# Clamping weight exponents on VectorE instead of ScalarE, wider spacing of the sums of second weights, and another order in the last product, in an fp32 attention and two-layer MoE kernel on one core

## The chip, the cores and the metric

The kernel runs on one NeuronCore of a Trainium2 chip, as one launch. The metric is the time of one launch on the device, in microseconds (us), as the median of several runs. TensorE is written PE, VectorE DVE, ScalarE ACT, GpSimd POOL and the queue that issues the transfers SP. PEld is PE's weight load, which runs beside its matmuls.

## The reference, cut to what matters

The inputs are `x` (4 batches, 8 heads, 512 tokens, 64 wide), a `state` of 32 tokens per batch, and the weights. TOK = 4 x (512 + 32) = 2176 tokens of 512 numbers go through the two layers.

```
a  = softmax(x @ state^T / 8);  xread = a  @ state
a2 = softmax(state @ x^T / 8);  sread = a2 @ x
x  = concat(xread, sread), heads side by side            # 2176 x 512
h  = x @ w_in                                            # 512 x 2048, float64
x  = (max(h, 0) + alpha * min(h, 0)) @ w_out             # 2048 x 512, float64
P  = exp(x @ w_gate - max), scaled 8 times by rows and columns
out = sum over 8 experts e of P[:, e] * (max(x @ w1[e], 0) @ w2[e])   # 512 x 1024 x 512
```

`w_in` and `w_out` are float64, so the kernel gets them as 64-bit words and has to make float32 of them on the chip. Each float32 product is made of three products of a shorter format: every operand is split into a high part and a low part (`...h`, `...l`), and high x high, high x low and low x high are summed in PSUM.

## The kernel before, in words

**Weights of the first layer.** F1 = 2048 is cut in eight steps u of 256. A step's weights, `w_in` and `w_out` together, are four pieces (u, j) of 128 x 512 words of 64 bits. `to_f32` (L98) turns one piece into float32 on three engines. DVE takes the exponent's bits out of the upper half word into `y` (L109) and later joins the lower bits (L115) and the sign (L123). ACT scales the low half word (L112) and clamps the exponent in three passes over `y`: max(y - 14336, 0) (L113), max(4095 - y, 0) (L119), and back times 2^19 (L120). POOL adds exponent and mantissa (L121). `split_w` (L129) then makes the high part on ACT (L138) and the low part on POOL (L139). There are 32 pieces.

**Start.** `start` (L1299) and the first part of the program (step 0, and step 1 up to the second product of the first batch) leave the order of each engine to a scheduler in the build. In this part run the attention of the four batches (`read_x`, L234) and the conversions of the first two steps. `read_x` of a batch makes the scores `psc` (L250), maxima and exponentials, sums (L271 to L273), the normalisation on POOL (L275), transposes `pat` (L282) whose halves go out on ACT and DVE (L230, L231), and then transposes `pst` (L295) for the softmax the other way. `pat` and `pst` share two PSUM banks, so `pst` waits until L231 has read `pat`.

**First layer.** From there on each engine follows the order of the code, which is dealt out in slots: a slot is a group of matmuls (`layer1` L503 or `layer2_first` L541), and after each slot every lane of side work (conversions `w`, attention `x`, and so on) takes one step. `layer1` is followed by ACT L527, DVE L530, ACT L535 and POOL L536, which make `gh` and `gl`. `layer2_first` fills a PSUM bank `po` (L551, three banks) and DVE adds it to the sum `acc` (L568). The conversion of step u + 1 is spread over step u by `weights` (L1276).

**Experts.** The 8 experts are 32 steps of 256, walked for each of three groups of tokens: 96 steps s. First products are done with seven smaller products (`quad`, `px`, `py`, `pz`, L850). Second products are plain in group 0 (L1167) and done with seven smaller products in groups 1 and 2 (`product`, L1023), from sums of second weights that are made in group 0 on ACT (L798) and DVE (L800) and kept in DRAM. For six steps these sums are made apart, in a lane of their own (`apart`, L815): it starts at step 6, and at step 26 what is left of it is done at once. `sums_b(u, raw, home, gap, rest)` (L776) takes `gap` and `rest` as the slots that it leaves free.

**The end.** `finish_last` (L1084) does the last second product plainly, joins the seven products' sums (five on DVE, two on POOL), transposes them and adds both. Tiles are cut where the six chunks of tokens end: (128, 128, 64) and (64, 128, 128) rows. Three tiles `pe` of the plain product run first, in three banks. Then come all transposes `pt`, each tile copied out by ACT (L1127), then the other three tiles of the plain product. DVE adds `pe` and the copy (L1109), and a transfer stores the tile.

Of the kernel before, what the change touches and what calls it, by code (L numbers as in the profile page):

```python
# [8 lines left out]
F32 = mybir.dt.float32  # L9
F32R = mybir.dt.float32r  # L10
I32 = mybir.dt.int32
# [3 lines left out]
AF = mybir.ActivationFunctionType  # L15
ALU = mybir.AluOpType
# [28 lines left out]
def body(ctx: ExitStack, tc: tile.TileContext, xt_in, xn_in, stb, stk, wd, ws, alpha, wgate, out):  # L45
# [22 lines left out]

    ident = const.tile([P, P], F32, name="ident")
    ones = const.tile([P, P], F32, name="ones")  # L70
    rebias = const.tile([P, 1], F32, name="rebias")
    full = const.tile([P, 1], F32, name="full")
    alpha_sb = const.tile([P, F1 // P], F32, name="alpha_sb")
    beta = const.tile([P, F1 // P], F32, name="beta")
    wg_raw = const.tile([P, KD, E], F32, name="wg_raw")
# [24 lines left out]
    def to_f32(u, j):  # L100

        w = raw_t[u, j].bitcast(I32).rearrange("p (n two) -> p n two", two=2)
        s = raw_t[u, j].bitcast(U16).rearrange("p (n four) -> p n four", four=4)
        lo_w, hi_w = w[:, :, 0], w[:, :, 1]
        y = rawp.tile([P, 512], F32, tag="y", name=f"y{u}_{j}", bufs=2)
        nc.vector.tensor_scalar(  # L109
            out=y.bitcast(I32), in0=hi_w, scalar1=16, scalar2=0x7FFF, op0=ALU.logical_shift_right, op1=ALU.bitwise_and  # L110
        )
        nc.scalar.activation(out=lo_w, in_=lo_w.bitcast(U32), func=AF.Copy, scale=2.0**-29)  # L112
        nc.scalar.activation(out=y, in_=y.bitcast(I32), func=AF.Relu, bias=rebias)  # L113
        yield
        nc.vector.scalar_tensor_tensor(  # L115
            out=lo_w, in0=s[:, :, 2], scalar=8.0, in1=lo_w, op0=ALU.mult, op1=ALU.add
        )

        nc.scalar.activation(out=y, in_=y, func=AF.Relu, scale=-1.0, bias=full)  # L119
        nc.scalar.activation(out=y.bitcast(I32), in_=y, func=AF.Copy, scale=-float(1 << 19), bias=4095.0 * (1 << 19))  # L120
        nc.gpsimd.tensor_tensor(out=lo_w, in0=y.bitcast(I32), in1=lo_w, op=ALU.add)  # L121
        yield
        nc.vector.scalar_tensor_tensor(  # L123
            out=lo_w, in0=hi_w, scalar=-0x80000000, in1=lo_w, op0=ALU.bitwise_and, op1=ALU.bitwise_or
        )
        src_t[u, j] = f32(lo_w)
# [688 lines left out]
    def apart():  # L815

        load_apart(None)
        yield 16
        for u in APART:
            yield from sums_b(u, raw_apart[u], "xl4", 2, 12)  # L820

    left2, whole = {}, {}

# [224 lines left out]
    def store(g, h, t0, nt, t):  # L1048

        tok = CH[2 * g + h][0] + t0  # L1050
        if tok < B * S:
            r0 = tok // S * (S + NS) + tok % S
            nc.sync.dma_start(out=out[r0:r0 + nt, :], in_=t[:nt])
        else:
            for b in range(B):
                r0 = b * (S + NS) + S
                nc.sync.dma_start(out=out[r0:r0 + NS, :], in_=t[b * NS:(b + 1) * NS])

    def cuts(g, h):

        t0, end = CH[2 * g + h][0], CH[2 * g + h][0] + CH[2 * g + h][1]
        at = t0
        while at < end:
            n = min(P, end - at, B * S - at if at < B * S else P)
            yield at - t0, n
            at += n
# [14 lines left out]
    def join(eng, g, x, y):  # L1081
        eng.tensor_tensor(out=mm[g][x], in0=mm[g][x], in1=mm[g][y], op=ALU.add)

    def finish_last(g):  # L1084

        s = NS2 - 1
        stage = big.tile([P, 6, DM], F32, tag="acc0", name="stage")
        gh, gl = g2[s]
        wh, wl = second[s]
        n = CH[2 * g][1]  # L1090
        parts = [(h, t0, nt) for h in range(2) for t0, nt in cuts(g, h)]

        def plain(i):
            h, t0, nt = parts[i]
            ps = ps_h.tile([P, 512], F32, tag="h", name=f"pe{i}")
            k = 0
            for f in range(NF):
                for x, w in ((gl, wh), (gh, wh), (gh, wl)):
                    nc.tensor.matmul(
                        ps[:nt], lhsT=x[:, f, h * n + t0:h * n + t0 + nt], rhs=w[:, f, :],  # L1100
                        start=(k == 0), stop=(k == 3 * NF - 1),
                    )
                    k += 1
            return ps

        def close(i, ps):
            h, t0, nt = parts[i]
            t = stage[:nt, i, :]
            nc.vector.tensor_tensor(out=t, in0=ps[:nt], in1=t, op=ALU.add)  # L1109
            store(g, h, t0, nt, stage[:, i, :])  # L1110

        for eng, x, y in (
            (nc.gpsimd, "P2", "P1"), (nc.gpsimd, "P3", "P5"), (nc.vector, "P6", "P1"), (nc.vector, "P7", "P6"),
            (nc.vector, "P4", "P7"), (nc.vector, "P3", "P6"), (nc.vector, "P7", "P5"),
        ):
            join(eng, g, x, y)
        first_ps = [plain(i) for i in range(3)]
        for i in range(0, 6, 2):
            ps = p2["m"].tile([P, 2, 512], F32, tag="m", name=f"pt{i}")
            for j in range(2):  # L1120
                h, t0, nt = parts[i + j]
                blocks = [("P2", "P4"), ("P3", "P7")][h]
                for k in range(KD):
                    nc.tensor.transpose(
                        ps[:nt, j, k * P:(k + 1) * P], mm[g][blocks[k // 2]][:, k % 2, t0:t0 + nt], ident
                    )
                nc.scalar.activation(out=stage[:nt, i + j, :], in_=ps[:nt, j], func=AF.Copy)  # L1127
        for i in range(3):
            close(i, first_ps[i])
        for i in range(3, 6):  # L1130
            close(i, plain(i))

    spread = {}

# [164 lines left out]
    def start():  # L1299
        load_b(0)  # L1300
        for j in range(2):
            load_w(0, j)
        make_identity(nc, ident)
        nc.vector.memset(ones, 1.0)
        nc.vector.memset(rebias, -14336.0)
        nc.vector.memset(full, 4095.0)
        warm(10)
        load_b(1)
        load_w(0, 2)
        load_b(2)  # L1310
        for j in range(2):
            load_w(1, j)
        load_b(3)
        load_w(1, 2)
        nc.sync.dma_start(out=alpha_sb, in_=alpha)
        nc.sync.dma_start(out=wg_raw, in_=wgate)

        x0, x1 = read_x(0), read_x(1)
        w0 = early([(0, j) for j in range(NPIECE)])
        for task in (x0, x1, x0, x0, w0, x0, w0, x0, w0, x0, w0):  # L1320
            next(task)
        for b in range(B):
            make_st2(b)
        next(w0)
        warm(30)
        nc.vector.tensor_scalar(out=beta, in0=alpha_sb, scalar1=-1.0, scalar2=1.0, op0=ALU.mult, op1=ALU.add)
        lanes["x"] += [x0, x1, read_x(2), read_x(3)]
        lanes["state"] += [states(b) for b in range(B)]
        lanes["w"] += [w0, early([(1, j) for j in range(NPIECE)])]
        lanes["v"] += [make_v(0), make_v(1)]  # L1330
# [201 lines left out]
```

## Time and profile before

| what | us |
|---|---|
| median of three runs (1857.4 to 1863.1) | 1859.85 |
| the profiled execution | 1864.35 |
| its span, first to last instruction | 1862.5 |
| PE busy in the span | 1791.9 (96%) |
| DVE busy | 1507.0 (81%) |
| POOL busy | 1252.4 (67%) |
| ACT busy | 732.8 (39%) |

The span is the stretch that the profiler's records cover; 1.85 us of the profiled execution lie outside it. Busy shares are means over the whole span: what an engine has free in one stage is read from windows of that stage. In the trace a row gives the start, the duration, the engine, the line of the kernel and the operands; in brackets stands how long the engine had been idle before it, and which instruction ended that.

### The profile page before, as it was taken

What the parts mean: (1) busy time and instruction counts of PE and PEld (TensorE: products, weight loads), DVE (VectorE), ACT (ScalarE), POOL (GpSimd) and SP (SyncE); (2) the same over time, 40 slices, a digit from 0 to 9 for tenths busy, and PEclk for the clock granted to TensorE, in tenths of its full rate; (3) what the DMA queues carried; (4) which work ended last, traced back from release to release, by engine and by line L of the source; (5) the groups of instructions that cost most, each with busy time, mean ns of one, the idle gap of its engine ahead of it and who ended that gap; (6) DMA issues with size and microseconds to landing.
All of it is one profiled execution on the core that took longest, in us unless ns stands there. A gap on an engine that the chain in (4) does not pass through costs nothing.

```text
span 1862.5 us, 29291 instructions
## 1 busy us (share of the span) xinstructions
PE 1791.9 (96%) x10173; PEld 1662.6 (89%) x10173; DVE 1507.0 (81%) x2318; ACT 732.8 (39%) x1394; POOL 1252.4 (67%) x1297
## 2 busy tenths in 40 slices
PE   6799999999989999999999999999999999999998
PEld 5688788877878888888889999999999999999997
DVE  6744777776899999998997777777788888877786
ACT  6755666654323443343332222222223333233332
POOL 4523555566667777787647777777776898677774
PEclk8899999999999999999999999999999999999998
DMA  6111111122659899898797677767777787888883
GB/s 221 46 52 46 57 46 57 46 74 84 235 210 332 329 331 326 321 333 299 271 332 271 252 269 269 256 254 250 266 263 266 265 308 278 325 312 315 296 305 106
DMA packets 153026, 427.20 MB, mean 229 GB/s; under 512 B 17312, under 2 KB 34208, under 8 KB 152880
## 3 DMA queue, kind: packets, MB, share of 16 engines
q1 hardware_dynamic: 152880, 425.34, 63.2%
q8 instruction: 81, 1.33, 0.3%
q14 instruction: 65, 0.53, 0.1%
HBM read 302.28 MB, written 122.99 MB: 228 GB/s over the span
## 4 chain that ended last, share of the span: by engine, by line
PE 69%; DVE 16%; POOL 4%; issue 4%; DMA 3%; ACT 3%; SPq 1%; DVEq 0%; POOLq 0%; ACTq 0%
PE pm L1023 22%; PE py L850 11%; PE px L850 8%; PE pz L850 8%; PE po L551 7%; PE po L1167 5%; PE ph L522 4%; DVE oa L1189 2%; DVE wz L800 2%; DVE g2l L873 1%; POOL w2l L672 1%; DMA kept_bs<-wz 1%; PE pv L484 1%; DVE c L857 1%; DMA rw<-in_ws_dram 1%
## 5 line engine op out<-in xcount | busy, mean ns | idle before, releaser
L1029 DVE TENSOR_TENSOR m<-pm,m 128x768 f32<-128x768 f32 (+1 forms) x427 | 377.9, 886 | 124.7 <-PE pm L1023 124.7
L1023 PE MATMUL pm<-formgh,wz 128*128 128x384 f32 (+1 forms) x1134 | 212.7, 322 | 0.4 <-DVE m L1029 0.4
L850 PE MATMUL px<-rB,wah 128*128 128x384 f32 (+1 forms) x768 | 189.9, 329 | 3.8 <-DVE g2l L873 3.5
L954 POOL TENSOR_TENSOR formgh<-mid,formgh 128x384 fp32r<-128x384 f32 (+1 forms) x126 | 121.2, 962 | 106.2 <-ACT formgh L953 106.1
L850 PE MATMUL py<-rT,wsh 128*128 128x384 f32 (+1 forms) x768 | 188.1, 327 | 0.2 <-DVE u L857 0.2
L1023 PEld LDWEIGHTS pm<-formgh,wz 128*128 128x128 f32 x1134 | 186.7, 188 | 0.7 <-issue 0.7
L672 POOL TENSOR_TENSOR w2l<-rw,w2h 128x512 fp32r<-128x512 f32 x64 | 87.0, 1381 | 127.9 <-ACT w2h L670 118.1
L536 POOL TENSOR_TENSOR gl<-r,gh 128x512 fp32r<-128x512 f32 (+1 forms) x80 | 94.3, 1192 | 114.8 <-ACT gh L535 60.2
L872 ACT ACTIVATE g2h<-c 128x384 fp32r<-128x384 f32 x96 | 50.5, 526 | 305.8 <-DVE c L857 305.8
L1167 PE MATMUL po<-w2l,g2h 128*128 128x512 f32 x384 | 152.4, 397 | 0.0
L1167 PE MATMUL po<-w2h,g2h 128*128 128x512 f32 x384 | 151.6, 395 | 0.0
L1167 PE MATMUL po<-w2h,g2l 128*128 128x512 f32 x384 | 150.0, 391 | 0.4 <-DVE g2l L873 0.4
L850 PEld LDWEIGHTS px<-rB,wah 128*128 128x128 f32 x768 | 135.7, 189 | 13.2 <-DVE g2l L873 8.1
L850 PEld LDWEIGHTS py<-rT,wsh 128*128 128x128 f32 x768 | 136.0, 188 | 3.6 <-DVE u L857 0.6
L964 POOL TENSOR_TENSOR T<-mid,mid 128x384 f32<-128x384 f32 (+1 forms) x126 | 118.0, 959 | 30.8 <-DVE mid L938 30.0
L953 ACT ACTIVATE formgh<-mid 128x384 fp32r<-128x384 f32 (+1 forms) x126 | 63.0, 500 | 178.1 <-DVE mid L938 134.2
L551 PE MATMUL po<-gl,wh 128*128 128x512 f32 (+1 forms) x320 | 120.1, 376 | 13.1 <-DVE acc L568 11.3
L1189 DVE SCALAR_TENSOR_TENSOR oa<-po,pr,oa 128x512 f32<-128x512 f32 x168 | 124.3, 740 | 6.8 <-PE po L1167 6.0
L938 DVE SCALAR_TENSOR_TENSOR mid<-mid,pb 128x384 f32<-128x384 f32 (+1 forms) x192 | 123.3, 642 | 6.6
L850 PE MATMUL px<-rB,wal 128*128 128x384 f32 (+1 forms) x384 | 125.6, 327 | 0.0
L850 PE MATMUL py<-rT,wsl 128*128 128x384 f32 (+1 forms) x384 | 125.2, 326 | 0.0
L1023 PE MATMUL pm<-formgl,w2h 128*128 128x384 f32 (+1 forms) x504 | 121.2, 323 | 3.4 <-DVE m L1029 1.9
(259 smaller groups left out, 5169.6 us busy)
## 6 DMA issues: line engine op xcount, KB each, us to landing
wz<-kept_bs SPq DMA_DIRECT2D x126, 512.0 KB, 8.1
kept_bs<-wz SPq DMA_DIRECT2D x64, 512.0 KB, 6.1
wsh<-kept_as_h SPq DMA_DIRECT2D x64, 512.0 KB, 3.7
wsl<-kept_as_l SPq DMA_DIRECT2D x64, 512.0 KB, 6.1
wah<-kept_a_h SPq DMA_DIRECT2D x64, 384.0 KB, 2.9
wal<-kept_a_l SPq DMA_DIRECT2D x64, 384.0 KB, 4.3
w2h<-kept_b_h SPq DMA_DIRECT2D x63, 384.0 KB, 6.5
w2l<-kept_b_l SPq DMA_DIRECT2D x63, 384.0 KB, 7.1
```

Of the source, the lines that this page charges most:

```text
L522: nc.tensor.matmul(ps, lhsT=w, rhs=x, start=(i == 0), stop=(i == len(terms) - 1))
L536: nc.gpsimd.tensor_tensor(out=lo, in0=r, in1=f32(hi), op=ALU.subtract)
L551: nc.tensor.matmul(ps, lhsT=w2(wt, u, f, d * P, P), rhs=g[:, f, :n], start=(i == 0), stop=(i == 3 * NF - 1))
L672: nc.gpsimd.tensor_tensor(out=lo[:, i], in0=src[:, i], in1=f32(hi[:, i]), op=ALU.subtract)
L850: nc.tensor.matmul(bank[b], lhsT=w[:, k * P:(k + 1) * P], rhs=xf[:, j, k, :], start=(first and i == 0), stop=(i == 5), skip_group_check=True,)
L938: nc.vector.scalar_tensor_tensor(out=out, in0=src, scalar=0.0, in1=pb[:, e % 2, h * n:(h + 1) * n], op0=ALU.max, op1=ALU.mult)
L954: nc.gpsimd.tensor_tensor(out=lo, in0=out, in1=f32(hi), op=ALU.subtract)
L964: nc.gpsimd.tensor_tensor(out=out, in0=x, in1=y, op=ALU.subtract)
L1023: nc.tensor.matmul(ps[:, q, :n], lhsT=w[:, q * P:(q + 1) * P], rhs=x, start=(j == 0), stop=(j == 2))
L1029: nc.vector.tensor_tensor(out=mm[g][name], in0=ps[:, :, :n], in1=mm[g][name], op=ALU.add)
L1167: nc.tensor.matmul(ps, lhsT=x[:, f, t * P:(t + 1) * P], rhs=w[:, f, :], start=(i == 0), stop=(i == 3 * NF - 1))
L1189: nc.vector.scalar_tensor_tensor(out=a, in0=ps, scalar=p, in1=a, op0=ALU.mult, op1=ALU.add)
```

## The change

It has three parts. In `to_f32` the three ACT passes over `y` give way to two integer passes on DVE, in place: add -14336 and take the larger of that and 0, then take the smaller of that and 4095 and multiply by 2^19. Two constants and their memsets go. In `apart` the slots left free are 4 and 14 in place of 2 and 12. `finish_last` does the plain product for five whole tiles of 128 rows first, copied out by ACT; the joins write one tile `blocks` with the rows side by side; then five tiles are transposed, and DVE adds each transposed bank to the copy. Five tiles are stored, the last by four transfers of 32 rows. Lines below the first part move up by 2.

```diff
@@ to_f32
-        nc.scalar.activation(out=y, in_=y.bitcast(I32), func=AF.Relu, bias=rebias)
+        yi = y.bitcast(I32)
+        nc.vector.tensor_scalar(out=yi, in0=yi, scalar1=-14336, scalar2=0, op0=ALU.add, op1=ALU.max)
         yield
         nc.vector.scalar_tensor_tensor(
             out=lo_w, in0=s[:, :, 2], scalar=8.0, in1=lo_w, op0=ALU.mult, op1=ALU.add
         )
-        nc.scalar.activation(out=y, in_=y, func=AF.Relu, scale=-1.0, bias=full)
-        nc.scalar.activation(out=y.bitcast(I32), in_=y, func=AF.Copy, scale=-float(1 << 19), bias=4095.0 * (1 << 19))
+        nc.vector.tensor_scalar(out=yi, in0=yi, scalar1=4095, scalar2=1 << 19, op0=ALU.min, op1=ALU.mult)
         nc.gpsimd.tensor_tensor(out=lo_w, in0=y.bitcast(I32), in1=lo_w, op=ALU.add)
@@ apart
-            yield from sums_b(u, raw_apart[u], "xl4", 2, 12)
+            yield from sums_b(u, raw_apart[u], "xl4", 4, 14)
@@ finish_last
-        stage = big.tile([P, 6, DM], F32, tag="acc0", name="stage")
+        t0, nt = GT[g]
+        stage = big.tile([P, nt, DM], F32, tag="acc0", name="stage")
+        whole_t = big.tile([P, KD, 2 * n], F32, tag="acc1", name="blocks")
+        def block(i, h):
+            return whole_t[:, 2 * i:2 * i + 2, h * n:(h + 1) * n]
+        for eng, to, x, y in (
+            (nc.gpsimd, block(0, 0), "P2", "P1"), (nc.gpsimd, m["P3"], "P3", "P5"), (nc.vector, m["P6"], "P6", "P1"),
+            (nc.vector, m["P7"], "P7", "P6"), (nc.vector, block(1, 0), "P4", "P7"),
+            (nc.vector, block(0, 1), "P3", "P6"), (nc.vector, block(1, 1), "P7", "P5"),
+        ):
+            eng.tensor_tensor(out=to, in0=m[x], in1=m[y], op=ALU.add)
...
-        first_ps = [plain(i) for i in range(3)]
-        for i in range(0, 6, 2):
...
-        for i in range(3):
-            close(i, first_ps[i])
-        for i in range(3, 6):
-            close(i, plain(i))
+        for t in range(nt):
+            ps = bank(("tr", "m", "h", "h", "h")[t], f"pe{t}")
...
+            nc.scalar.activation(out=stage[:, t, :], in_=ps, func=AF.Copy)
+        for t in range(nt):
+            ps = bank(("m", "tr", "m", "h", "h")[t], f"pt{t}")
+            for k in range(KD):
+                nc.tensor.transpose(ps[:, k * P:(k + 1) * P], whole_t[:, k, t * P:(t + 1) * P], ident)
+            row = stage[:, t, :]
+            nc.vector.tensor_tensor(out=row, in0=ps, in1=row, op=ALU.add)
...
+                nc.sync.dma_start(out=out[r0:r0 + P, :], in_=row)
```

Three places show how it moves instructions. A row names line, operation, result and operands. In the names `raw1_3` is piece (1, 3), `wl` a low half of weights, `r1_0` the row sums of batch 1, and `early_a`, `early_b` hold the pieces (1, 0) to (1, 2) and the exponentials of the batches 0 and 1.

POOL in the start, before, from the piece (0, 2) on:

```order
L139 TENSOR_TENSOR wl0_2_386<-raw0_2_136,wh0_2_385 128x512
L275 TENSOR_TENSOR early_b_102<-early_b_102,r1_0_473 128x512
L275 TENSOR_TENSOR early_b_102<-early_b_102,r1_1_478 128x512
L214 TENSOR_TENSOR stl_100<-xt3_0_145,sth_99 128x2x64 x2
L121 TENSOR_TENSOR raw0_3_252<-y0_3_259,raw0_3_252 128x512
L121 TENSOR_TENSOR early_a_101<-y1_0_427,early_a_101 128x512
L139 TENSOR_TENSOR wl0_2_386<-raw0_3_252,wh0_2_385 128x512
L121 TENSOR_TENSOR early_a_101<-y1_1_435,early_a_101 128x512
L139 TENSOR_TENSOR wl1_0_449<-early_a_101,wh1_0_448 128x512
L121 TENSOR_TENSOR early_b_102<-y1_2_444,early_b_102 128x512
L139 TENSOR_TENSOR wl1_0_449<-early_a_101,wh1_0_448 128x512
L121 TENSOR_TENSOR raw1_3_281<-y1_3_457,raw1_3_281 128x512
```

And POOL at the same place with the change (L119, L137, L273 and L534 are the former L121, L139, L275 and L536):

```order
L119 TENSOR_TENSOR raw0_3_246<-y0_3_252,raw0_3_246 128x512
L119 TENSOR_TENSOR early_a_99<-y1_0_419,early_a_99 128x512
L137 TENSOR_TENSOR wl0_2_378<-raw0_3_246,wh0_2_377 128x512
L119 TENSOR_TENSOR early_a_99<-y1_1_426,early_a_99 128x512
L137 TENSOR_TENSOR wl1_0_439<-early_a_99,wh1_0_438 128x512
L119 TENSOR_TENSOR early_b_100<-y1_2_434,early_b_100 128x512
L137 TENSOR_TENSOR wl1_0_439<-early_a_99,wh1_0_438 128x512
L273 TENSOR_TENSOR early_b_100<-early_b_100,r1_0_461 128x512
L119 TENSOR_TENSOR raw1_3_274<-y1_3_446,raw1_3_274 128x512
L137 TENSOR_TENSOR wl1_2_597<-early_b_100,wh1_2_596 128x512
L273 TENSOR_TENSOR early_b_100<-early_b_100,r1_1_466 128x512
L534 TENSOR_TENSOR gl0_0_336<-r0_0_1_391,gh0_0_335 128x512
```

The two normalisations of batch 1 (`r1_0`, `r1_1`), which stood ahead of the conversions from (0, 3) on, now stand behind seven and nine instructions of conversions; the second half of `gl0_0` stands right behind them.

PE in the start, before, from batch 1's transposes on:

```order
L282 MATMUL pat1_0_483<-ident_87,early_b_102 128x128 x4
L282 MATMUL pat1_1_490<-ident_87,early_b_102 128x128 x4
L295 MATMUL pst1_0_497<-ident_87,sc1_0_402 128x128 x2
L295 MATMUL pst1_0_497<-ident_87,sc1_1_403 128x128 x2
L295 MATMUL pst1_1_506<-ident_87,sc1_0_402 128x128 x2
L295 MATMUL pst1_1_506<-ident_87,sc1_1_403 128x128 x2
L250 MATMUL psc2_0_515<-xt2_0_138 128x64 x8
L551 MATMUL po0_0_0_645<-gl0_0_344,wh0_2_385 128x512
L551 MATMUL po0_0_0_645<-gh0_0_343,wh0_2_385 128x512
```

And with the change (L280, L293 and L549 are the former L282, L295 and L551):

```order
L549 MATMUL po0_0_2_685<-gh0_0_335,wl0_2_378 128x512
L280 MATMUL pat1_0_471<-ident_87,early_b_100 128x128 x2
L280 MATMUL pat1_1_478<-ident_87,early_b_100 128x128 x2
L280 MATMUL pat1_0_471<-ident_87,early_b_100 128x128 x2
L280 MATMUL pat1_1_478<-ident_87,early_b_100 128x128 x2
L549 MATMUL po0_0_0_633<-gl0_0_336,wh0_2_377 128x512
L549 MATMUL po0_0_0_633<-gh0_0_335,wh0_2_377 128x512
L549 MATMUL po0_0_0_633<-gh0_0_335,wl0_2_378 128x512
L549 MATMUL po0_0_1_660<-gl0_0_336,wh0_2_377 128x512
L549 MATMUL po0_0_1_660<-gh0_0_335,wh0_2_377 128x512
L549 MATMUL po0_0_1_660<-gh0_0_335,wl0_2_378 128x512
L549 MATMUL po0_0_2_685<-gl0_0_336,wh0_2_377 128x512
```

Three tiles' first halves of `po0_0` (nine matmuls) now stand ahead of `pat1`, and seven matmuls that need the second half of `gl0_0` ahead of `pst1`. Batch 2's scores, which followed `pst1`, now come behind all 24 matmuls of this chunk.

DVE in the first layer, at the piece (4, 1), before:

```order
L109 TENSOR_SCALAR y4_1_2061<-raw4_1_1817 128x512
L530 SCALAR_TENSOR_TENSOR r3_1_1_2058<-r3_1_1_2058,beta_92,ph3_1_1_2051 128x512
L568 TENSOR_TENSOR acc0_679<-po3_0_0_2065,acc0_679 128x512
L115 SCALAR_TENSOR_TENSOR raw4_1_1817<-raw4_1_1817 128x512
L568 TENSOR_TENSOR acc0_679<-po3_0_1_2075,acc0_679 128x512
L568 TENSOR_TENSOR acc0_679<-po3_0_2_2089,acc0_679 128x512
L123 SCALAR_TENSOR_TENSOR raw4_1_1817<-raw4_1_1817 128x512
```

And with the change (L107, L114, L121, L528 and L566 are the former L109, L115, L123, L530 and L568):

```order
L107 TENSOR_SCALAR y4_1_2040<-raw4_1_1798 128x512
L112 TENSOR_SCALAR y4_1_2040<-y4_1_2040 128x512
L528 SCALAR_TENSOR_TENSOR r3_1_1_2037<-r3_1_1_2037,beta_90,ph3_1_1_2030 128x512
L566 TENSOR_TENSOR acc0_667<-po3_0_0_2044,acc0_667 128x512
L114 SCALAR_TENSOR_TENSOR raw4_1_1798<-raw4_1_1798 128x512
L118 TENSOR_SCALAR y4_1_2040<-y4_1_2040 128x512
L566 TENSOR_TENSOR acc0_667<-po3_0_1_2054,acc0_667 128x512
L566 TENSOR_TENSOR acc0_667<-po3_0_2_2067,acc0_667 128x512
L121 SCALAR_TENSOR_TENSOR raw4_1_1798<-raw4_1_1798 128x512
```

Two passes over `y` (L112 and L118) are added for the piece. Both stand ahead of additions (L566) that free a bank of `po` for PE.

## Rows read from the trace of the kernel before

**Rows 1.** The page, its part 4: the chain that ended last, shares by engine.

```profile
PE 69%; DVE 16%; POOL 4%; issue 4%; DMA 3%; ACT 3%; SPq 1%; DVEq 0%; POOLq 0%; ACTq 0%
```

**Rows 2.** Waits of PE, 0 to 100 us: total us, times, longest.

```profile
PE pst L295 <- DVE al L231: 16.9, 3, 15.0
```

**Rows 3.** Timeline 27 to 57 us: start, us, instruction, [idle before <-what ended it].

```profile
27.72 2.05 POOL L275 TENSOR_TENSOR early_b<-early_b,r 128x512 f32<-128x512 f32 x2 [0.27 <-DVE r L273]
...
41.91 1.29 POOL L121 TENSOR_TENSOR raw<-y,raw 128x512 int32<-128x512 int32 x1 [10.98 <-ACT y L120]
...
38.95 0.63 PE L282 MATMUL pat<-ident,early_b 128*128 128x128 f32 x4 [2.29 <-DVE al L497]
54.57 1.11 PE L295 MATMUL pst<-ident,sc 128*128 128x128 f32 x4 [14.99 <-DVE al L231]
...
53.83 0.68 DVE L231 TENSOR_TENSOR al<-pat,ah 128x512 fp32r<-128x512 f32 x1
```

**Rows 4.** Four lines: ns min/median/max, start of first and last, form.

```profile
L109 DVE TENSOR_SCALAR y<-raw x29: 408/430/1511, 10.5 to 374.1; 128x512 int32<-128x512 int32 x29
...
L115 DVE SCALAR_TENSOR_TENSOR raw<-raw x29: 676/686/1778, 12.0 to 378.8; 128x512 int32<-128x512 uint16 x29
...
L121 POOL TENSOR_TENSOR raw<-y,raw x29: 1282/1304/1807, 14.4 to 380.1; 128x512 int32<-128x512 int32 x29
...
L119 ACT ACTIVATE y<-y,full x32: 706/709/744, 12.6 to 377.9; 128x512 f32<-128x512 f32 x32
```

**Rows 5.** Timeline around 51 and 228 us, DVE and POOL.

```profile
50.72 1.76 DVE L123 SCALAR_TENSOR_TENSOR early_a<-early_a 128x512 int32<-128x512 int32 x1 [2.73 <-POOL early_a L121]
...
50.64 1.29 POOL L139 TENSOR_TENSOR wl<-early_a,wh 128x512 fp32r<-128x512 f32 x1
...
228.37 1.21 DVE L109 TENSOR_SCALAR y<-raw 128x512 int32<-128x512 int32 x1
237.02 1.22 DVE L109 TENSOR_SCALAR y<-raw 128x512 int32<-128x512 int32 x1
...
227.98 1.32 POOL L139 TENSOR_TENSOR wl<-raw,wh 128x512 fp32r<-128x512 f32 x1 [1.50 <-ACT wh L138]
```

**Rows 6.** Windows: length; busy PE, PEld, DVE, ACT, POOL; clock, DMA, GB/s.

```profile
200.00:220.00 20.00, 20.00 (x111) 17.26 (x110) 16.19 (x27) 11.29 (x21) 8.62 (x8) 1.00 0.18 54
240.00:260.00 20.00, 20.00 (x110) 17.27 (x110) 16.93 (x30) 13.07 (x25) 11.23 (x10) 1.00 0.16 52
280.00:300.00 20.00, 20.00 (x113) 17.38 (x112) 17.74 (x32) 14.75 (x28) 10.51 (x9) 1.00 0.17 54
320.00:340.00 20.00, 20.00 (x113) 17.44 (x112) 17.43 (x30) 15.09 (x26) 11.05 (x9) 1.00 0.15 53
```

**Rows 7.** The waits of PE from 100 to 440 us.

```profile
PE po L551 <- DVE acc L568: 11.3, 8, 3.2
```

**Rows 8.** Window of the stage with the second weights' sums.

```profile
600.00:800.00 200.00, 195.76 (x969) 172.28 (x968) 198.11 (x287) 80.34 (x148) 150.85 (x160) 1.00 0.90 326
```

**Rows 9.** Timeline of the last 25 us, PE, DVE and the store queue.

```profile
1838.02 0.39 PE L1099 MATMUL pe<-w2h,g2xh 128*128 128x512 f32 x1
...
1838.25 0.39 PE L1099 MATMUL pe<-w2h,g2xl 128*128 128x512 f32 x1
...
1840.92 4.65 DVE L1082 TENSOR_TENSOR m<-m,m 128x640 f32<-128x640 f32 x5
...
1844.15 0.44 PE L1124 MATMUL pt<-ident,m 128*128 128x128 f32 x2 [1.63 <-DVE m L1082]
...
1853.97 0.69 DVE L1109 TENSOR_TENSOR stage<-pe,stage 128x512 f32<-128x512 f32 x1 [5.76 <-PE pe L1099]
...
1857.77 0.69 DVE L1109 TENSOR_TENSOR stage<-pe,stage 128x512 f32<-128x512 f32 x1 [0.70 <-PE pe L1099]
1858.49 1.74 SPq L1057 DMA_DIRECT2D out_dram<-stage  x4
```

**Rows 10.** Window in the last tiles.

```profile
1851.30:1854.00 2.70, 2.70 (x8) 1.90 (x7) 0.03 (x1) 0.60 (x1) 0.00 (x0) 0.50 0.00 0
```

More of the change, by code (lines that the diff above doesn't have):

```diff
@@ L70, in body @@
     ones = const.tile([P, P], F32, name="ones")
-    rebias = const.tile([P, 1], F32, name="rebias")
-    full = const.tile([P, 1], F32, name="full")
     alpha_sb = const.tile([P, F1 // P], F32, name="alpha_sb")
@@ L1090, in finish_last, with bank @@
         n = CH[2 * g][1]
[L1091 to L1095, printed above, removed]
+        m = mm[g]
+        whole_t = big.tile([P, KD, 2 * n], F32, tag="acc1", name="blocks")
[7 more added lines that the diff above has]
+            eng.tensor_tensor(out=to, in0=m[x], in1=m[y], op=ALU.add)
+        def bank(kind, name):
+            if kind == "m":
+                return p2["m"].tile([P, 2, 512], F32, tag="m", name=name)[:, 0]
+            return (p2["tr"] if kind == "tr" else ps_h).tile([P, 512], F32, tag=kind, name=name)
+        for t in range(nt):
+            ps = bank(("tr", "m", "h", "h", "h")[t], f"pe{t}")
             k = 0
@@ L1099, in plain @@
                     nc.tensor.matmul(
-                        ps[:nt], lhsT=x[:, f, h * n + t0:h * n + t0 + nt], rhs=w[:, f, :],
-                        start=(k == 0), stop=(k == 3 * NF - 1),
+                        ps, lhsT=x[:, f, t * P:(t + 1) * P], rhs=w[:, f, :], start=(k == 0), stop=(k == 3 * NF - 1)
                     )
                     k += 1
[L1104 to L1116, printed above, removed]
-        first_ps = [plain(i) for i in range(3)]
-        for i in range(0, 6, 2):
[L1119 to L1127, printed above, removed]
-        for i in range(3):
-            close(i, first_ps[i])
-        for i in range(3, 6):
-            close(i, plain(i))
+            nc.scalar.activation(out=stage[:, t, :], in_=ps, func=AF.Copy)
[5 more added lines that the diff above has]
+            nc.vector.tensor_tensor(out=row, in0=ps, in1=row, op=ALU.add)
+            if t < nt - 1:
+                r0 = (t0 + t) // 4 * (S + NS) + (t0 + t) % 4 * P
+                nc.sync.dma_start(out=out[r0:r0 + P, :], in_=row)
+            else:
+                for b in range(B):
+                    r0 = b * (S + NS) + S
+                    nc.sync.dma_start(out=out[r0:r0 + NS, :], in_=row[b * NS:(b + 1) * NS])
     spread = {}
@@ L1304, in start @@
         nc.vector.memset(ones, 1.0)
-        nc.vector.memset(rebias, -14336.0)
-        nc.vector.memset(full, 4095.0)
         warm(10)
```

## The prediction

> **What bounds the kernel now.** I read the page's chain of waits first, then PE's waits by stage, then the windows and the timelines of those places. The chain [rows 1] is 69% PE and 16% DVE: an engine that is off that chain, as ACT mostly is with 3%, gives nothing back by itself when work leaves it. The reader should therefore ask at each place who makes PE wait. In the first 100 us it is one wait, `pst` behind L231 [rows 2], 14.99 us of it in one piece that ends at 54.57 [rows 3]: the subtraction at 53.83 that frees the bank stands on DVE behind conversions of weights, and these hang on POOL (L123 idle 2.73 behind L121, [rows 5]). From 100 to 440 us PE waits 11.3 us in 8 places for the additions L568 [rows 7], so DVE is late there though its windows show 2 to 4 us free in 20 [rows 6]. In the stage with the sums DVE is full: 198.11 of 200 us, and PE has 4.24 us idle [rows 8]. At the end PE waits for a join and DVE for PE in turn [rows 9], and the clock is at its lower level of 1.2 GHz, granted 0.50 [rows 10].
>
> **What leaves ACT.** 32 pieces lose three passes each, 96 x 0.71 = 68 us by L119's row [rows 4]. Nothing waits for ACT there in the long run, so I cost this at nothing but for the start: there the chain of passes holds POOL idle for 10.98 us until 41.91 [rows 3]. With DVE's short passes I let that conversion begin at about 40, as an estimate, 2 us earlier.
>
> **What comes to DVE.** 64 passes with one source, both ends in SBUF, 128 x 512 int32. The nearest row is L109, the same form and type: 0.43 median, 1.51 at most [rows 4]. Far off is L115 with two operands, 0.69, which I keep as the upper bound for a pass alone. The maximum of L109 matters. At 228.37 it took 1.21 while POOL's L139 ran from 227.98 to 229.30, and it ended 0.28 after it; at 50.72 L123 took 1.76 under another L139 in place of 0.69 [rows 5]. So a DVE operation that reads and writes SBUF waits for a POOL operation that is under way. The Trainium skill (SBUF — State Buffer, section SBUF: two separate sides) has this as an exclusive lock on a port pair which VectorE and GpSimd share: whichever starts first keeps it for its whole instruction. The rows above agree with it; by the rule the new passes are not worth their 0.43, and without it the parts below on the start and the first layer would come to about zero.
>
> **Start.** The order shown decides: batch 1's normalisations L275, done by 29.77 before [rows 3], now stand on POOL behind the conversions. From about 40 to the end of the second of them POOL has nine conversion operations of 1.28 (L121's shortest, L139 alike) and two of 1.03 (2.05 for two, [rows 3]), 13.6 us. DVE's port operations between them, taken one after another with them, are some ten one-source passes of 0.43, 4.3, and six two-operand ones of 0.69, 4.1 [rows 4]. That is 22.0, to 62.0. `gl0_0`'s second half is one more POOL operation, to 63.3. Seven matmuls follow it ahead of `pst`. After an idle stretch I take the lower clock for them, twice the pitch of 0.23 (1838.02 to 1838.25, [rows 9]): 7 x 0.46 = 3.2, to 66.5. That is 11.9 after 54.57. The transposes `pat`, 0.63, two ACT copies and two L231 of 0.68 [rows 3] fit between 62.0 and 66.5. Of what then has to be done, 16 matmuls of `po0_0` are already behind PE; at the full clock's pitch of 0.23 that returns 3.7. But batch 2's scores now come behind all 24 matmuls, so what hangs on them starts some 8 x 0.23 = 1.8 later; I count 1 of it. Sum: 11.9 - 3.7 + 1 = 9.2, **+9**. Bounds: if POOL and DVE do not hold each other up, POOL ends at 40 + 13.6 + 1.3 = 55, and net of the returned 3.7 the start may gain 4; if nothing is returned it loses 13.
>
> **First layer.** Pieces come every 8.65 us inside a step (228.37, 237.02, [rows 5]), so two in 20 us. Both new passes of a piece stand among operations of POOL that follow each other; I add to each 1.0, about what the two caught rows lost (1.21 - 0.43 and 1.76 - 0.69), and take 0.35 rather than 0.43 since successive operations overlap. So 2 x 2 x 1.35 = 5.4 per 20 us. DVE has free in the four heavy windows [rows 6] 3.81, 3.07, 2.26 and 2.57 us. The excess is 1.6 + 2.3 + 3.1 + 2.8 = 9.8, and each microsecond of it is an addition L568 that comes late to PE [rows 7], because PE is full there (20.00 of 20). About 1 more comes from 100 to 200 us: **+11**. The lighter windows between them take the rest, so that nothing is carried on. Bounds: 0, if the passes run unhindered (4 x 0.43 = 1.7, below the free 2.26); and +19, if a pass has L115's 0.69 as well: 4 x 1.69 = 6.8 less the free times gives 3.0 + 3.7 + 4.5 + 4.2 = 15.4, and some 3 from before 200 us.
>
> **Sums apart.** The two numbers spread the same operations over 42 slots a step in place of 34, still inside group 0. DVE is full there [rows 8] and its total stays, so only the clustering can matter: of the 4.24 us that PE is idle I give back 1, **-1**. Bounds: -4 (all of it) and +2 (the last step lands where the first products of the next group start).
>
> **The end.** PE runs 30 plain matmuls from 1838.02 without a break, to 1838.02 + 30 x 0.23 = 1844.9; ACT's copies (0.6 each) lie beside them. The joins are the same and end at 1840.92 + 4.65 = 1845.57. The 20 transposes (0.22 each, 0.44 for two, [rows 9]) start as the joins end and keep ahead of DVE, so that DVE's five additions bound it: 5 x 0.69 = 3.45, to 1849.0. Before, the last addition ended at 1857.77 + 0.69 = 1858.46: the end comes 9.4 earlier. The stores behind the last addition are the same four transfers, 4.0 us to the end of the span (1862.5), though four larger stores now stand close ahead on the queue, up to 0.5. I take **-9**; -8 if the transposes run at twice 0.22 in the lower clock and so bound DVE, -10 at best. DVE's wait of 5.76 for the second three tiles [rows 9] is what goes.
>
> **Sum.** 9 + 11 - 1 - 9 = +10, against the profiled execution 1864.35, so 1874.35. That execution lies 4.5 above the median of 1859.85; on the median's scale I forecast 1859.85 + 10 = 1869.85, **1870 us**. 0.3% of it is 5.6 us, about what a measurement of this kernel can tell from no change; so "same" is 1854.3 to 1865.4.
>
> **Rivals.**
> - *A faster start and room on DVE (other side).* What ACT loses pulls the start forward by its bound of 4, the passes fit into DVE's free time, the end gives 9, the sums 1: -14, **1846 us**. For it speaks that POOL sat idle 10.98 us behind ACT [rows 3], that the new passes may fall between POOL operations, and that DVE shows free time in every window [rows 6]. It decides if the second L275 of batch 1 ends before about 52. Against it: [rows 5], and the place of that L275 in the order. 0.13.
> - *The passes do not contend, but the start's order costs.* Start +9, first layer +2, sums -1, end -9: +1, **1861 us**. For it: most L109 (median 0.43, [rows 4]) were not caught. 0.2.
> - *Slow passes and the contention.* The first layer at its bound of 19 and the start at 13, sums -1, end -9: +22; with additions held up by conversions in the lighter windows too, up to +27; between the two **1884 us**. For it: integer arithmetic with two operations shows in no row, since L109 is shift and mask. 0.07.
>
> **How the numbers follow.** The forecast, +5 to +19 with the bounds of its terms, has 0.6; its lower end lies at 1865, so a little of it counts as same. Low end 1856 takes in the rival at 1861 with its spread and leaves the fast one out (0.13); high end 1880 leaves the slow one out (0.07). Faster 0.13; same 0.2, the second rival nearly whole and a little of the forecast; slower 0.67.
>
> **What would show it.** Right: `pst`'s long wait ends near 66 in place of 54.57, with L273 of batch 1 behind L119 on POOL; in the windows from 200 to 340 us PE drops below 20.00 by 1 to 3 each and its waits for L566 grow from 11.3 to about 22; L112 and L118 show minima near 0.41 and maxima over 1.2; the last addition ends about 11 us after the first plain matmul of `pe0`, instead of 20.4. Wrong: PE is as full in these windows as now, or `pst` ends its wait before 55. Then the first terms fall, and the time is that of the first or second rival.

## The result and the profile of the changed kernel

The changed kernel takes 1871.2 us (median, 1870.68 to 1874.12) and the kernel before, timed with it, 1858.62 (1857.27 to 1863.1): 1.0059 times as long, 95% interval 1.0039 to 1.0080. Timed again in another set of runs (e5 below) it is 1873.0 against 1861.25, 1.0054 (1.0037 to 1.0071). The ratios here and below are those on record, with their intervals; dividing the two medians would give 1.0068 and 1.0063.

The two profiled executions are nearer to each other, 1868.8 against 1862.5 us of span. Cut at instructions that both have (start of the first, the 21st and the last addition into `acc`, first addition to the sums `m` of the seven products, first plain matmul of the last product):

| stretch | before | changed | difference |
|---|---|---|---|
| to the first addition | 89.29 | 98.48 | +9.19 |
| first to 21st addition | 95.25 | 92.18 | -3.07 |
| 21st to last addition | 255.96 | 269.83 | +13.87 |
| to the first addition to the seven products' sums | 557.91 | 553.89 | -4.02 |
| to the first plain matmul | 839.61 | 839.37 | -0.24 |
| to the end of the span | 24.48 | 15.05 | -9.43 |

PE's waits from 0 to 100 us and from 100 to 440, which answer to [rows 2, 7] (total us, times, longest):

```profile
PE pat L280 <- POOL early_b L273: 16.3, 3, 11.6
PE po L549 <- POOL gl L534: 7.6, 2, 7.3
...
PE po L549 <- DVE acc L566: 17.4, 9, 3.1
```

The start's long wait is no longer for L231 but for POOL's normalisation itself. Its timeline, as [rows 3]:

```profile
42.89 1.74 POOL L119 TENSOR_TENSOR raw<-y,raw 128x512 int32<-128x512 int32 x1
...
61.32 1.50 POOL L273 TENSOR_TENSOR early_b<-early_b,r 128x512 f32<-128x512 f32 x1
62.78 1.44 POOL L534 TENSOR_TENSOR gl<-r,gh 128x512 fp32r<-128x512 f32 x1
...
62.87 1.11 PE L280 MATMUL pat<-ident,early_b 128*128 128x128 f32 x4 [3.29 <-POOL early_b L273]
...
67.20 0.60 PE L293 MATMUL pst<-ident,sc 128*128 128x128 f32 x4
```

The second normalisation ends at 62.82 and `pst` begins at 67.20. The windows of [rows 6], and the two new lines (ns, min/median/max):

```profile
200.00:220.00 20.00, 20.00 (x108) 17.21 (x107) 19.05 (x33) 11.73 (x21) 11.03 (x8) 1.00 0.17 53
240.00:260.00 20.00, 18.53 (x84) 15.58 (x85) 19.16 (x32) 10.33 (x18) 10.60 (x8) 0.91 0.15 50
280.00:300.00 20.00, 17.17 (x81) 14.00 (x80) 19.00 (x27) 8.11 (x15) 11.76 (x9) 1.00 0.15 52
320.00:340.00 20.00, 17.53 (x82) 14.38 (x82) 16.66 (x23) 8.50 (x15) 11.03 (x9) 0.91 0.09 27
```

```profile
L112 DVE TENSOR_SCALAR y<-y x32: 407/428/1553, 11.2 to 395.3; 128x512 int32<-128x512 int32 x32
...
L118 DVE TENSOR_SCALAR y<-y x32: 357/423/1520, 12.8 to 399.0; 128x512 int32<-128x512 int32 x32
```

In the first of these windows PE is as full as before, in the other three it is not, and in two the granted clock falls to 0.91. Part of this lies in where the windows are cut: the wait of a step ends at 230.90, 273.52 and 316.11 before, outside them, and at 241.47, 286.64 and 331.99 now, inside. The passes run at L109's rate alone and up to 1.55 beside POOL. The place where one of the waits is made, timeline around 240 us:

```profile
237.39 1.21 DVE L107 TENSOR_SCALAR y<-raw 128x512 int32<-128x512 int32 x1
...
237.86 0.62 ACT L533 ACTIVATE gh<-r 128x512 fp32r<-128x512 f32 x1
...
238.61 1.27 POOL L534 TENSOR_TENSOR gl<-r,gh 128x512 fp32r<-128x512 f32 x1 [0.30 <-POOL wl L137]
238.62 1.53 DVE L112 TENSOR_SCALAR y<-y 128x512 int32<-128x512 int32 x1
...
240.08 0.73 DVE L528 SCALAR_TENSOR_TENSOR r<-r,beta,ph 128x512 f32<-128x512 f32 x1
240.74 0.68 DVE L566 TENSOR_TENSOR acc<-po,acc 128x512 f32<-128x512 f32 x1
...
241.47 0.79 PE L549 MATMUL po<-gl,wh 128*128 128x512 f32 x1 [2.46 <-DVE acc L566]
```

This is the piece (4, 1) of the change's section. L112 begins 0.01 after POOL's L534 and runs until that has ended (239.88); the leak L528 (the step that makes `r`, of which ACT and POOL make `gh` and `gl`) and the addition L566 stand behind it, and PE waits 2.46 for the bank. Before, the same wait was 1.21 (at 230.90). There is one such wait in each step, five in all, and each grows from 1.2 to 2.46. The end, as [rows 9]:

```profile
1853.75 0.39 PE L1113 MATMUL pe<-w2h,g2xh 128*128 128x512 f32 x1
...
1860.59 2.34 PE L1121 MATMUL pt<-ident,blocks 128*128 128x128 f32 x20
...
1861.29 3.08 DVE L1123 TENSOR_TENSOR stage<-pt,stage 128x512 f32<-128x512 f32 x5
1862.01 2.16 SPq L1126 DMA_DIRECT2D out_dram<-stage  x4
1864.40 1.73 SPq L1130 DMA_DIRECT2D out_dram<-stage  x4
```

30 matmuls, 20 transposes and five additions follow without a wait, the last addition ends at 1864.37, 10.62 after the first matmul, where it was 20.44.

### The profile page after: what moved, and what is told of

Read it like the earlier page. It is cut to its first block, busy times and chain, and to the rows that moved or that the text cites. A ratio compares the mean times of both kernels' runs of the same rounds, so it can differ in the third digit from the quotient of the medians.

```text
span 1868.8 us, 29165 instructions
## 1 busy us (share of the span) xinstructions
PE 1794.3 (96%) x10163; PEld 1669.4 (89%) x10163; DVE 1548.7 (83%) x2379; ACT 676.1 (36%) x1297; POOL 1262.6 (68%) x1297
## 4 chain that ended last, share of the span: by engine, by line
PE 81%; DVE 12%; POOL 2%; issue 2%; ACT 2%; DMA 1%; DVEq 0%; POOLq 0%; ACTq 0%
PE pm L1021 22%; PE py L848 14%; PE po L1166 11%; PE px L848 9%; PE pz L848 9%; PE po L549 7%; PE ph L520 4%; PE pv L482 1%; DVE oa L1188 1%; POOL raw L119 1%; DVE y L112 1%; PE psr L327 1%; POOL gl L534 1%; DVE wz L798 1%; DVE r L528 1%
## 5 line engine op out<-in xcount | busy, mean ns | idle before, releaser
L534 POOL TENSOR_TENSOR gl<-r,gh 128x512 fp32r<-128x512 f32 (+1 forms) x80 | 96.2, 1211 | 125.3 <-ACT gh L533 109.6
L549 PE MATMUL po<-gl,wh 128*128 128x512 f32 (+1 forms) x320 | 122.4, 382 | 26.8 <-DVE acc L566 17.4
```

The lines of the kernel that those rows point to most:

```text
L534: nc.gpsimd.tensor_tensor(out=lo, in0=r, in1=f32(hi), op=ALU.subtract)
L549: nc.tensor.matmul(ps, lhsT=w2(wt, u, f, d * P, P), rhs=g[:, f, :n], start=(i == 0), stop=(i == 3 * NF - 1))
```

## The experiments

In each of three sets (e1 to e4, e5 to e8, e9 to e12) the kernels ran on one chip beside the kernel before. Stretches are cut as in the table; "the stage" is the one from the 21st to the last addition. Lines of a kernel with an edit ahead of them are shifted.

**The parts alone.** Run e1 is the `to_f32` part of the diff on the kernel before, e2 the `finish_last` part, e3 the `apart` line, e4 both of these without `to_f32`.

> The kernel before with the first part of the change alone: the three ACT passes of the exponent clamp give way to two DVE passes. Theory A (the prediction's sum, term by term): +9 in the start and +11 in the first layer, nothing later, so +20, about 1879 us; the first addition into acc starts near 98 us and the last near 460, against 89.3 and 440.5 before. Rival B (the terms lie elsewhere: the start is disturbed but the first layer's loss comes with the other parts of the change): +9, about 1868, last addition near 450. Rival C (the relief of ACT counts, and the loss of the whole change comes from the end or the sums): 0 or faster.

Measured: 1.0070 (1.0049 to 1.0092), 1878.37 against 1865.22. First addition at 97.35, 21st at 189.42, last at 459.15: the stage takes 269.73. Theory A's places hold, its sum of +20 does not: the ratio gives +13 us (9 to 17).

> The kernel before with the new order of the last product alone. Theory A: -9, about 1850 us; from the first plain matmul to the last addition's end 11 us in place of 20.4, and nothing else moves. Rival B (the stores' queue takes back part, or the clock falls during the transposes): -6 to -8, with 12 to 14 us from the first plain matmul to the last addition.

Measured: 0.9930 (0.9906 to 0.9954), 1853.52 against 1865.22; 10.61 us from the first plain matmul to the last addition's end. Theory A's place holds. The ratio gives -13 us (-18 to -9), so the -9 forecast lies at the edge of the interval.

> The kernel before with the wider spacing of the second weights' sums alone (4 and 14 in place of 2 and 12). Theory A (prediction): -1, so 1857 to 1858, same. Rival B (the 4.2 us that disappeared between 440 and 998 us in the profile of the changed kernel come from this spacing): -4, about 1854.5, and PE's waits for DVE between 440 and 1000 us fall from 11.4 us to about 7. Rival C (they are a chance difference between two executions): 0, with the same waits.

Measured: 1.0013 (0.9994 to 1.0033). PE waits 12.7 us between the last addition and 1000 us, and the stretch to the seven products takes 558.40. Over all profiles of this study that stretch took 551.8 to 557.9 in ten executions with the old spacing and 553.9 to 558.4 in four with the new. The 4 us in the first table are within that scatter, and the interval leaves out rival B's -4: rival C.

> The change without its first part: the ACT passes stay, the spacing and the last product are the new ones. Theory A: -9 and -1 add up, about 1849 us, clearly under the kernel before. Rival B of the spacing run: -13, about 1845.5. If the parts interact (the spacing only pays where the start is late), the sum differs from the two single runs by more than 2 us.

Measured: 0.9959 (0.9943 to 0.9975). The end takes 10.61 to the last addition and the stage 255.83, as in e2 and before. The ratio gives -8 us (-11 to -5), where Theory A had -10. The intervals of e2 and e4 overlap a little, so whether the spacing costs something is not settled. Both e2 and e4 are faster than the kernel before; which of the two is better is not shown.

**Once more, and the steps apart.** Run e5 is the changed kernel. In e6 `to_f32` chooses by `u >= 3`:

```diff
-        nc.scalar.activation(out=y, in_=y.bitcast(I32), func=AF.Relu, bias=rebias)
+        yi = y.bitcast(I32)
+        if u >= 3:
+            nc.vector.tensor_scalar(out=yi, in0=yi, scalar1=-14336, scalar2=0, op0=ALU.add, op1=ALU.max)
+        else:
+            nc.scalar.activation(out=y, in_=y.bitcast(I32), func=AF.Relu, bias=rebias)
```

and likewise at the second pass.

> The changed kernel once more, timed on the same chip as the kernel before. If the parts simply add up (first part alone +13, last product alone -12, spacing between 0 and +2): +1 to +4. If the first result (ratio 1.0059) holds on every chip: +11. In its profile the stage from the 21st to the last addition into acc should again take 269 to 270 us, and the end from the first plain matmul on 15 us.

Measured: 1.0054, +10 us (7 to 13), so not the +1 to +4 of the parts. The stage took 267.39, the end 10.62.

> The kernel before with the DVE passes for the steps u = 3 to 7 only; the steps 0 to 2, and so the whole start, keep the ACT passes. Theory A (the first layer's loss is made there, by the DVE passes of these steps): from the 21st to the last addition into acc 269 to 270 us as with the whole first part, against 256 to 257 before; start as before (first addition at 89 to 94); +13 in all. Rival (the loss is handed on from the start): under 260 us in that stage, and +2 or less in all.

Measured: 1.0090 (1.0069 to 1.0111), +17 us where +13 was expected, the stage 272.36, the first addition at 94.14. The first layer's loss is made there and not handed on.

**What on DVE makes the loss.** Runs e7 and e8 keep the ACT passes and call `more(u)` ahead of L113 and of L119, for `u >= 3` on a spare tile:

```diff
+        nc.vector.tensor_scalar(out=i, in0=i, scalar1=0, scalar2=0, op0=ALU.add, op1=ALU.max)   # e7
+        nc.vector.tensor_reduce(out=extra[1], in_=extra[0], axis=AX.X, op=ALU.max)              # e8
```

> The kernel before, ACT passes kept, with two more DVE passes per piece for u = 3 to 7: integer passes of the same form as the new ones, over a spare tile of 128 x 512, at the places of the new ones. They change nothing of the result. Theory A (the passes on DVE make the loss, not the shorter chain on ACT): 269 us from the 21st to the last addition, within 2 us. Rival (it is the changed times at which ACT, DVE and POOL finish a piece): about 257 us, as before.

Measured: 1.0049 (1.0024 to 1.0074), the stage 265.38. Two passes more lose 9 us of the 12.5 that the stage loses with the change (worked out below) although ACT keeps its own, so passes on DVE are enough for most of the loss. It is not made in the same way, though. PE's idle time is as long as in the changed kernel (265.38 - 246.21 = 19.2), in more and shorter waits: 6 of the 9. The rest is busy time (246.21 against 242.88 before) at an unchanged clock, whose cause is not shown; the granted clock of the stage stays at 0.99:

```profile
190.82:456.20 265.38, 246.21 (x1251) 204.12 (x1250) 218.37 (x342) 150.99 (x268) 141.12 (x120) 0.99 0.15 49
```

The wait of each step is 1.54 to 1.73 here, not 2.46. Its place in step 4:

```profile
236.87 1.22 DVE L120 TENSOR_SCALAR y<-raw 128x512 int32<-128x512 int32 x1
...
238.02 0.42 DVE L109 TENSOR_SCALAR scr<-scr 128x512 int32<-128x512 int32 x1
...
238.76 1.14 ACT L548 ACTIVATE gh<-r 128x512 fp32r<-128x512 f32 x2
...
239.50 1.29 POOL L549 TENSOR_TENSOR gl<-r,gh 128x512 fp32r<-128x512 f32 x1 [1.69 <-ACT gh L548]
```

ACT makes `gh` behind its own pass, POOL's `gl` comes at 239.50, and the pass on DVE is over by then. In the changed kernel ACT has no pass there: `gh` begins 0.47 after L107 (237.86 and 237.39, in the timeline above) and not 1.89 after it, as here (238.76 - 236.87), and `gl` begins just ahead of L112. So ACT's shorter chain does have a part in the change's longer waits.

> As the run with two more passes, but each of the two is a maximum over the spare tile of 128 x 512 into 128 x 1: it reads one operand from SBUF and takes 0.68 us by the rows of L271, longer than an undisturbed pass of 0.43, and in the profile of the changed kernel such a reduction at 51.52 us ran 0.67 us beside a POOL operation that began at 51.53. Theory A (a pass costs what it waits behind POOL, so 1.94 us for the two passes of a piece): a piece gets 1.3 us on DVE, which is inside its free time, and the stage takes 257 to 261 us. Rival B (it is DVE's time alone that counts, 0.86 us a piece undisturbed): the loss is larger than with the passes, 271 us or more.

Measured: 1.0062 (1.0044 to 1.0081), the stage 265.49. Both theories miss. The reductions were not held up once:

```profile
L109 DVE TENSOR_REDUCE top<-scr x40: 671/674/686, 182.7 to 392.8; 128x1 f32<-128x512 f32 x40
```

12 of them began while a POOL operation ran, and they cost as much as the passes of e7. So an operation need not be held to make a loss. DVE's sum of time is not excluded by this: the reductions take 0.67 in the mean of 38, and the passes of e7, some of which were held, 0.71. The place was left to test.

**The place.** Run e9 is e6 with `u < 3` in place of `u >= 3`. e10 keeps only the first of e8's two calls, e11 only the second. e12 is e6 with the second pass moved up behind the first:

```diff
         if u >= 3:
             nc.vector.tensor_scalar(out=yi, in0=yi, scalar1=-14336, scalar2=0, op0=ALU.add, op1=ALU.max)
+            nc.vector.tensor_scalar(out=yi, in0=yi, scalar1=4095, scalar2=1 << 19, op0=ALU.min, op1=ALU.mult)
...
         yield
...
-        if u >= 3:
-            nc.vector.tensor_scalar(out=yi, in0=yi, scalar1=4095, scalar2=1 << 19, op0=ALU.min, op1=ALU.mult)
-        else:
+        if u < 3:
```

> The kernel before with the DVE passes for the steps u = 0 to 2 only, so with the start's new order, and ACT passes from step 3 on. The prediction's term: +9 in all, about 1872 us where the kernel before has 1863. What the profiles with and without the first part suggest: PE is idle 34.5 us up to the 21st addition into acc in place of 31.9, and the first addition comes some 5 later, but 5 of it are back by the 21st, because one wait of 2.5 us near 163 us and the low clock behind it are gone; so 0 to +3 in all, and 256 to 257 us from the 21st to the last addition.

Measured: 1.0016 (1.0001 to 1.0030), 21st addition at 189.48, stage 256.49. The start costs about 3 us (0.2 to 6), not 9.

> The kernel before with one more reduction (0.68 us, not held by POOL) per piece for u = 3 to 7, at the place of the first of the new passes. If DVE's free time in the windows absorbs work until it is used up, as the prediction reckoned (two pieces in 20 us make 1.4 us, under the 2.26 to 3.8 that are free): 256 to 258 us from the 21st to the last addition. If each microsecond that a piece adds on DVE ahead of the additions costs PE a share of itself (two reductions cost 9 us for some 30 us of DVE): 260 to 262 us.

> The same single reduction at the place of the second of the new passes, behind L115. Free time absorbs it: 256 to 258 us. A share of each microsecond: 260 to 262 us. If the place decides (the first stands ahead of L115 and pushes it into POOL's time, the second does not): under 258 here and over 262 with the first place.

Each of the two ran once: 1876.35 and 1860.68 us, against 1861.83 for the kernel before. Windows over the stage of e10, then of e11 (columns as in [rows 6]):

```profile
186.31:455.77 269.46, 253.28 (x1250) 211.96 (x1250) 207.06 (x324) 152.23 (x268) 138.69 (x120) 0.95 0.15 49
```

```profile
184.26:441.86 257.60, 243.97 (x1252) 203.75 (x1251) 197.64 (x324) 150.78 (x268) 138.46 (x120) 0.99 0.16 51
```

Against the 256.5 of the kernels without it, the same reduction costs 13 us at the first place and 1 at the second, so DVE's sum of time does not decide. The 13 is one execution: e8, which has the reduction at both places, lost 9. PE's idle time repeats better: 16.2 in e10, 16.4 in e8, 13.6 in e11. Behind L115 the reduction delays no addition that PE waits longer for: the five waits of e11 stay at 1.2. At the first place it stands, once a step, ahead of the leak and the addition that frees PE's bank:

```profile
232.34 1.21 DVE L120 TENSOR_SCALAR y<-raw 128x512 int32<-128x512 int32 x1
...
233.47 0.68 DVE L109 TENSOR_REDUCE top<-scr 128x1 f32<-128x512 f32 x1
234.07 0.73 DVE L542 SCALAR_TENSOR_TENSOR r<-r,beta,ph 128x512 f32<-128x512 f32 x1
234.72 0.68 DVE L580 TENSOR_TENSOR acc<-po,acc 128x512 f32<-128x512 f32 x1
235.32 1.47 DVE L127 SCALAR_TENSOR_TENSOR raw<-raw 128x512 int32<-128x512 uint16 x1
235.46 0.50 PE L563 MATMUL po<-gl,wh 128*128 128x512 f32 x1 [1.80 <-DVE acc L580]
```

The wait is 1.80 here (e11: 1.20), 0.60 longer, which is the time from the reduction's start to the next operation's (233.47 to 234.07). It comes five times. Of the 11.9 us between e10 and e11, 2.6 are PE's idle time (269.46 - 253.28 against 257.60 - 243.97); the other 9.3 are its busy time, 253.28 for the matmuls that took 243.97, at a granted clock of 0.95 in place of 0.99.

> The kernel before with both DVE passes for u = 3 to 7 one right behind the other, ahead of the first pause, in place of the second one two slots later. In the runs before the second pass was the one that POOL held most (mean 1.17 us, 13 of 19 over 1 us; the first 0.89). If what POOL holds back makes the loss: the second pass falls to about 0.5 us, and the stage from the 21st to the last addition to 262 us or less, against 267 to 272. If the waiting only moves on to the next operation (as to L115 in the run with reductions): 267 us or more.

Measured: 1.0110 (1.0081 to 1.0139), stage 278.04. The second pass was held less (median 0.43) and the loss grew, since now both stand ahead of that addition: the wait is 3.07 (at 237.36). Of the two forecasts the second held, for a reason that neither named.

## Why the prediction was right

The forecast of 1870 us held: +10 was written, and 12.6 and 11.8 measured (by the medians). Its terms held less well than the sum, so part of the hit is luck: the start was put at +9 and gives about 3, and the terms as measured add up to some +5, further from the result than the forecast.

**Start, +9.** The mechanism is as written, nearly to the microsecond: normalisation over at 62.82 (62.0 written), `gl` at 64.22 (63.3), `pst` at 67.20 (66.5), the first addition 9.19 later. The step that failed is the sum, "11.9 - 3.7 + 1", which ended at that place. Over all profiles of this study the first addition came at 91.3 in the mean of ten starts in the old order and at 97.4 in four in the new, and the 21st at 187.9 and 189.6: of 6.1 us 4.4 are given back. One thing that was not looked for gives back: a wait of 2.5 us for the subtraction L497 at 162 to 165 us, with a granted clock of 0.66 in the 5 us behind it, of which 0.7 is left in the changed kernel. The wait is 2.4 to 2.6 in all ten starts in the old order and 0.6 to 0.7 in the four in the new.

```profile
164.81 0.36 PE L484 MATMUL pv<-wl,sth 128*128 128x256 f32 x1 [2.50 <-DVE al L497]
```

```profile
165.00:170.00 5.00, 5.00 (x25) 4.48 (x25) 3.02 (x6) 3.15 (x8) 2.99 (x3) 0.66 0.47 133
```

(both of the kernel before.) The text ahead of the prediction puts the end of the scheduler's part too early; it is the first product of step 2, at 174.73, so this place belongs to it. Run e9 gives 3 us (0.2 to 6) for the whole term, inside its bounds of -4 and +13, and leaves out its +9.

**First layer, +11.** Measured 12.5: 269.0 in the mean of e1, e5 and the first profile, 256.5 in five with ACT passes and nothing added (e6, with the DVE passes in this stage, took 272.4). The size is right, the working is not. The two passes take 0.80 and 1.15 us in the mean of the 21 that begin after 100 us, not 1.35 each. DVE's free time in a window is no cushion: e10 adds 0.6 us per piece, far inside it, and loses 13 (e8, with two of 0.6, 9). The windows of [rows 6] show PE full only because they lie between the waits of 1.2 us that the kernel before has in each step. What decides is the one addition in a step that PE waits for. Its wait grows by 1.25, five times 6.3 us: that is PE's idle time, 13.1 before (255.96 - 242.88) and 19.2 after (269.83 - 250.62). The other 7.7 us are the same matmuls at a lower clock, which the prediction did not have at all:

```profile
184.54:440.50 255.96, 242.88 (x1252) 204.00 (x1251) 186.52 (x304) 150.91 (x268) 138.49 (x120) 0.99 0.16 51
```

```profile
190.66:460.49 269.83, 250.62 (x1253) 209.79 (x1252) 222.85 (x342) 115.61 (x211) 140.42 (x120) 0.96 0.14 48
```

This is also why L566's waits came to 17.4 and not to the 22 that were to show the step right. That a pass waits out the POOL operation under way held: L112 at 238.62 shows it, and it is why the wait grows by 1.25 here and by 0.35 in e7, where the pass took 0.42. The Trainium skill (SBUF — State Buffer, section SBUF: two separate sides) lets only operations that use the shared ports wait; the 40 reductions with one operand, 671 to 686 ns, agree.

**Sums apart, -1.** Not distinguishable from 0 (e3).

**End, -9.** 9.43 in the first profile. Up to the last addition the new order takes 10.6 us in each of the four kernels that have it, the old one 16.5 to 20.5 in ten. The clock stayed at its upper level (granted 1.00 from 1853.75 to 1864.40), and the four larger stores cost 0.3 to 0.4 (4.4 us from the last addition to the end of the span, 4.1 before).

**What leaves ACT, nothing.** This term failed. With the passes gone ACT makes `gh` earlier, and POOL's `gl` comes to stand right ahead of the new pass (238.61 and 238.62). The same is seen at all five places of the five kernels in which ACT has no pass there: the first pass takes 1.51 to 1.54. In e7, where ACT keeps its passes, it takes 0.41 to 0.42. So the prediction had the new passes held by POOL, but not that ACT's relief moves POOL there. How the 12.5 us divide between the two is not shown: no run relieves ACT without adding to DVE.

**The rivals.** The faster start needed the second normalisation before about 52; it ended at 62.82. That the passes do not contend is refuted by L112 at 238.62 and by its maximum of 1553 ns, that they are slow by nature by the minima of 407 and 357 ns.

**Open.** Terms from the profiles add up to some +5 (1.7 + 12.5 - 9.4), the three parts timed alone to +0.1% with an uncertainty of about 0.4, e1 and e4, which together are the whole change, to +0.3% with 0.3, and the whole to +0.54 and +0.59%. So the parts may well add up; that they interact is not shown. The executions scatter by as much: in two starts of the same instructions in the same order PE was busy 152.46 and 159.39 us up to the 21st addition, idle 32.1 and 31.6, at clocks of 0.91 and 0.87.

```profile
0.00:184.54 184.54, 152.46 (x920) 133.48 (x921) 109.57 (x192) 117.11 (x228) 71.90 (x68) 0.91 0.27 92
```

```profile
0.00:190.94 190.94, 159.39 (x920) 139.85 (x921) 109.56 (x192) 117.29 (x228) 71.90 (x68) 0.87 0.26 89
```

(the kernel before, and e2.) The execution that the prediction worked from had one of the shortest starts seen. A term of a few microseconds in the start can't be read from one profile of each kernel; where the rest of the gap lies, if it is more than scatter, stays open.

## What to carry to other kernels

On an engine that works in order, an added operation costs by what stands right behind it, not by the engine's free time: find the wait that recurs, see which instructions stand between its releaser and the last thing that released it, and count only what lands there. Where work has to be added, put it behind that instruction (1 us here) and not ahead of it (9 to 13 us). Where work is taken off an engine, ask what it now does earlier, and what that runs into: here ACT's earlier `gh` put POOL's `gl` in front of the new pass. Read a loss on TensorE in two halves, idle time and busy time at the granted clock, and compare stages between several executions before a difference of a few microseconds is given a cause.

## What was not expected of the hardware

The price of a short wait. Five waits that grew from 1.2 to 1.8 us (e11 to e10, one execution each) came with 9.3 us more of PE's busy time, and with a granted clock of the stage of 0.95 in place of 0.99. Not every longer wait has this price. Of the waits at these five places, over all profiles of this study, none of the 35 between 1.15 and 1.73 us was followed within 2 us by the lower clock, those of e7 among them; of the 35 between 1.79 and 3.20 us, 24 were. What decides among those is not shown. The window behind the changed kernel's wait at 241.47 is one of the 24:

```profile
240.00:250.00 10.00, 8.53 (x32) 6.97 (x33) 9.35 (x14) 3.56 (x7) 5.13 (x4) 0.83 0.16 49
```
